# Loading order, weight layout and block schedule at the start of a fused attention and mixture-of-experts kernel

## The chip, the cores and the metric

The kernel runs on one core of a Trainium2 chip. The metric is device time in microseconds (us) of one execution, lower is better. The engines are TensorE (PE, matrix products; "PEld" in the profile is its loading of weights), VectorE (DVE), ScalarE (ACT), GpSimd (POOL) and SyncE (SP, which here only issues DMAs); ACT and POOL issue DMAs too. On each engine instructions run in program order.

## The reference

Three steps: a linear attention with a decaying state, a first feed-forward step with `h - tanh(h)`, and a second one with eight experts. Cut to what matters:

```python
# attention: batch 4, heads 8, sequence 768, head dimension 48
f = 1.0 / (1.0 + np.exp(-f_logit))
for t in range(S):
    state = f[:, :, t, :, None] * state + np.einsum('bhd,bhde->bhde', k[:, :, t], v[:, :, t])
    y[:, :, t] = np.einsum('bhd,bhde->bhe', q[:, :, t], state)
# first feed-forward step: x is 3072 x 384, w_in 384 x 2048, w_out 2048 x 384
h = x @ w_in
g = h - np.tanh(h)
x = g @ w_out
# second step: the tokens with x @ w_skip > 0 go to the best of 8 experts
# (w1 384 x 1024, w2 1024 x 384 each) and add gate_w * (relu(x @ w1[e]) @ w2[e])
```

The weights `w_in` and `w_out` arrive as 64-bit floats, seen by the kernel as pairs of 32-bit words.

## The kernel before

**Attention** goes through 24 units u; a unit is 128 tokens of one batch, u = 4 · chunk + batch, all 8 heads. For a unit SP loads `f`, `k`, `q`, `v` (L262, L275). ACT and DVE make the logarithm of the decay (exp L279, min L282, ln L286); PE sums it along the tokens (`pl`, L387); ACT takes two exponentials of that (`kp` L396, `en` L400), by which DVE scales k and q (L403, L406); PE turns both (`pk`, `pq`, L416) and ACT copies them out (`kT`, `qT`, L423). Then PE makes the scores (`ps`, L437) and adds the state's part (`py`, L446), DVE masks the scores (`A`, L460), and PE multiplies them with v ("values", L472) and makes the state's update (`pu`, L479), which DVE adds to the state S (L512). The last row of `en` goes by a DMA on ACT (L409, put_dec) to a table `dec` in DRAM; for each pair of units two DMAs (L517, on ACT) bring two rows of it back, laid out by partition, as `dd`, with which POOL decays S (L522) and DVE checks the range (`okd`, L527). `dec` is preset with ones: POOL fills `one` (L726), and SP writes it (L727), inside the first function of the program. Two units make a block of 256 tokens (`xf`), which ACT and DVE split into two parts (`xT`, L533, L537).

**First feed-forward step.** 12 blocks; the inner dimension of 2048 is 16 f-blocks of 128. For a block and an f-block: gemm1, called G (`ph`, L596, 9 matmuls), tanh (L603, ACT), the difference, called bend (L608, DVE), its split (`gs`, L613 on ACT, L619 on POOL), gemm2, called H (`po`, L636, 6 matmuls). Blocks 0, 1 and 2 run interleaved from the f-block NJOIN on; before that block 0 runs alone up to NJOIN, then 1, then 2. H of blocks 1 and 2 sums in the PSUM banks of `py` and `ps`, and waits for values 7.

**Weights.** `w_in` and `w_out` come in four quarters each (`stgw`, `stgu`, L193, two buffers in turn: w0, u0, w1, u1, ...). A quarter is decoded in four chunks of 128x768 each: |u| on ACT (L168), four steps on DVE (L170, L172, L174, L178), the high part on ACT (L339), the low part on DVE (`wlo`, `ulo`, L343). A G of f-block f needs the low part of `w_in`'s chunk f // 2. A quarter of `w_in` goes to partitions 0 to 47 and 64 to 111 (48 each) and 48 to 63 and 112 to 127 (16 each), by the order in which the heads lie in `xT`.

**What sets the order.** All instructions ahead of the last two blocks are written as steps, `step(key, due time, engine, cost, function, what it stands behind, ..., moved)`, and a planner (`in_order`, L47 to L103) emits, each time, the step that can begin first by these costs, by due time where several can. A step takes and gives PSUM buffers; each pool has two (`pa`, `yp`, `po`, `ph`). Constants: units below FIRST are prepared one by one; NJOIN, see above; CHUNK0 and CHUNK are the due times of decoding; LDAFTER is the unit behind whose q the weights may be asked for; units below ALONE take `pl` from pool `ph` and `pk`, `pq` from `po`, all others take them from `pa`, which also holds `ps` and `pu`:

```python
pl_in, pk_in = ("ph", "po") if u < ALONE else ("pa", "pa")
```

Of the kernel before, what the change touches and what calls it, by code (L numbers as in the profile page):

```python
# [92 lines left out]
def decay_attention_moe_kernel(  # L93
# [14 lines left out]
    nc = tc.nc  # L108
    P = 128
# [4 lines left out]
    NU = NCH * B  # L114
# [12 lines left out]
    AHEAD = 2  # L127
    FIRST, NJOIN, NPAY = 8, 8, 6
    EARLIEST, LEAD = -100, 28
    LDAFTER, ALONE = 4, 6  # L130
    CHUNK0, CHUNK = -75, 4
    LAG = 2
# [50 lines left out]
    def fetch(pool, name, shape, pieces, dst, eng):  # L183

        n = pieces[0][3]
        if n == 2 or dst is None:
            t = pool.tile(shape + [2], I32, tag="stg", name=f"stg{name}")
        if n == 2:
            to = t.rearrange("p a w c -> p a (w c)")
        else:  # L190
            to = t = t.bitcast(F32)[..., 0] if dst is None else dst
        for rows, a, src, _ in pieces:
            eng.dma_start(to[rows, a], src)  # L193
        return t
# [101 lines left out]

    def load_win(j):
        w = DFF // NWL
        src, m = words(w_in)
        cs = slice(j * w * m, (j + 1) * w * m)  # L300
        rows = src[:, cs].rearrange("(h r) c -> h r c", r=D)
        pieces = []
        for jj, (h0, h2, h3) in enumerate(((0, 5, 7), (4, 1, 3))):
            o = 64 * jj
            pieces.append((slice(o, o + D), slice(0, 2), rows[h0 : h0 + 3 : 2].rearrange("h r c -> r h c"), m))
            pieces.append((slice(o, o + D), slice(2, 3), rows[h2 : h2 + 1].rearrange("h r c -> r h c"), m))
            pieces.append((slice(o + D, o + 64), slice(0, 3), rows[h3].rearrange("(i r) c -> r i c", r=16), m))
        stage["w", j] = fetch(spool, f"w{j}", [P, KT, w], pieces, None, nc.sync)

    def load_wout(j):  # L310
        n = NF // NWL
        src, m = words(w_out)
        stage["u", j] = fetch(
            spool, f"u{j}", [P, n, DM],
            [(slice(0, P), slice(0, n), src[j * n * P : (j + 1) * n * P].rearrange("(f p) d -> p f d", p=P), m)],
            None, nc.sync,
        )
# [45 lines left out]
    def attend(u):  # L363
# [9 lines left out]
        def at(pos):  # L373
            return (NF * blk - LEAD if u > FIRST - 1 else EARLIEST + 12 * blk) + 6 * half + pos
# [174 lines left out]
        step(("mq", u), at(1), "DVE", 0.56, mq, ("en", u), ("q", u), ("tq", u - 2))  # L549
        step(("put_dec", u), at(1), "ACT" if u < FIRST else "SP", 0.6, put_dec, ("en", u), moved=0.1)  # L550
        step(("tk", u), at(1), "PE", 0.44, turn4("k", kp4), ("mk", u), ("init", 0), take=((pk_in, f"k{u}"),), lag=0.25)
# [163 lines left out]
    def initial():  # L715
# [10 lines left out]
        nc.gpsimd.memset(one, 1.0)  # L726
        nc.sync.dma_start(dec, one[:NU].rearrange("u p a -> u (p a)"))  # L727

# [169 lines left out]

    step(("init", 0), -400, "POOL", 3.0, initial, moved=0.1)
    step(("const", 0), 0, "POOL", 3.0, constants, ("init", 0), moved=1.0)  # L900
    step(("turn", 0), -1000, "PE", 0.4, lambda: turned.append(turn_gate()), ("const", 0), ("scores", 2), take=(("pa", "gate"),), lag=0.25)
    step(("rows", 0), -1000, "ACT", 0.5, copy_gate, ("turn", 0), give=(("pa", "gate"),))
# [8 lines left out]
    for n, (a, j) in enumerate(chunks):  # L911
        at = CHUNK0 + CHUNK * n
        if n % 2 == 0:
            step(
                ("ld", n), at - 20, "SP", 2.7 if a == "w" else 0.45, (lambda a=a, j=j: (load_win if a == "w" else load_wout)(j // 2)),
                ("stt2", n - 3), ("q", LDAFTER), moved=9.2 if a == "w" else 4.5,
            )
# [498 lines left out]
```

## Time and profile before

| | us |
|---|---|
| median of 3 runs | 752.26 (752.19 to 753.14) |
| profiled execution | 752.0 |
| its span, first to last instruction | 750.1 |
| TensorE busy in the span | 694.7 (93%) |
| VectorE busy in the span | 498.1 (66%) |

The page gives the busy time of each engine. The table of waits says for which engine or DMA an engine stood still, the timelines list single instructions with the idle time before them in brackets and what ended it, the table of stretches gives each engine's busy time between two points of the span, and the DMA view gives what the transfers of a stretch moved. "PEclk" is the clock that TensorE was granted, as a share of full speed.

### The profile page before, as it was taken

The numbers are of one execution on the slowest core, as the hardware profiler recorded it, in microseconds if no ns is written. First come the engines' busy times: TensorE is split into PE (matmuls) and PEld (weight loads), VectorE is DVE, ScalarE is ACT, GpSimd is POOL, SyncE is SP. The second block draws the span as 40 slices with busy tenths as digits, with TensorE's granted clock in tenths as the row PEclk, the third lists the DMA queues.
The fourth block names the chain that finished last, engine by engine and source line by source line (L and its number), as shares of the span: only waits on it lengthen the run. The fifth ranks groups of instructions, "written<-read, shape, count | busy, mean of one in ns | idle before, by whom it ended". The sixth has DMA issues, their size and how long they took to land. (4 is left out here: it accounts for less than half of the span.)

```text
span 750.1 us, 16375 instructions
## 1 busy us (share of the span) xinstructions
PE 694.7 (93%) x6128; PEld 655.0 (87%) x6128; DVE 498.1 (66%) x1388; ACT 366.1 (49%) x864; POOL 284.5 (38%) x317
## 2 busy tenths in 40 slices
PE   3857989999999999989999999999989989999993
PEld 2646888899998999989899999999989779999993
DVE  2448989842887947688989594955665655555530
ACT  2656575544656445554444644444333525555530
POOL 2113234443333434344343443434444214444451
PEclk9987999999999999999999999999999999999998
DMA  7978975352432223202233112005000667666500
GB/s 141 168 161 154 204 162 93 98 183 82 102 69 54 60 44 74 50 17 54 54 82 63 45 35 43 28 7 197 11 32 18 229 210 217 224 213 206 169 18 21
DMA packets 150575, 76.78 MB, mean 102 GB/s; under 512 B 116360, under 2 KB 145689, under 8 KB 150358
## 3 DMA queue, kind: packets, MB, share of 16 engines
q1 hardware_dynamic: 143318, 70.37, 37.1%
q0 software_dynamic: 2944, 5.05, 2.0%
q10 hardware_dynamic: 4224, 0.22, 0.5%
q8 instruction: 50, 0.82, 0.5%
q14 instruction: 39, 0.32, 0.1%
HBM read 61.61 MB, written 15.87 MB: 103 GB/s over the span
## 5 line engine op out<-in xcount | busy, mean ns | idle before, releaser
L619 POOL TENSOR_TENSOR gs<-th,gs 128x256 fp32r<-128x256 f32 x190 | 168.4, 889 | 240.5 <-ACT gs L613 228.2
L636 PE MATMUL po<-uhi,gs 128*128 128x384 f32 x768 | 231.0, 344 | 2.8 <-POOL gs L619 2.1
L596 PE MATMUL ph<-xT,whi 128*128 128x256 f32 x1152 | 222.4, 289 | 4.5 <-DVE th L608 4.0
L596 PEld LDWEIGHTS ph<-xT,whi 128*128 128x128 f32 x1152 | 185.8, 191 | 11.1 <-DVE th L608 7.3
L596 PE MATMUL ph<-xT,wlo 128*128 128x256 f32 x576 | 164.0, 285 | 1.7 <-DVE wlo L343 1.7
L636 PEld LDWEIGHTS po<-uhi,gs 128*128 128x128 f32 x768 | 142.7, 190 | 7.0 <-POOL gs L619 4.4
L209 DVE CUSTOM_DVE_ANT_0 scr<-pay,wb 128x384 f32<-128x384 f32 x198 | 134.2, 678 | 5.5 <-ACT pay L644 1.7
L608 DVE TENSOR_TENSOR th<-ph,th 128x256 f32<-128x256 f32 x192 | 80.1, 419 | 85.8 <-ACT th L603 84.0
L636 PE MATMUL po<-ulo,gs 128*128 128x384 f32 x384 | 130.2, 339 | 1.6 <-DVE ulo L343 1.6
L603 ACT ACTIVATE th<-ph 128x256 f32<-128x256 f32 x192 | 73.0, 381 | 118.0 <-PE ph L596 83.3
L613 ACT ACTIVATE gs<-th 128x256 fp32r<-128x256 f32 x192 | 79.6, 416 | 90.4 <-DVE th L608 85.4
L596 PEld LDWEIGHTS ph<-xT,wlo 128*128 128x128 f32 x576 | 110.8, 192 | 2.1 <-DVE wlo L343 2.1
L636 PEld LDWEIGHTS po<-ulo,gs 128*128 128x128 f32 x384 | 73.5, 191 | 2.4 <-DVE ulo L343 2.4
L1079 PE MATMUL eh<-xt,w 128*128 128x256 f32 x504 | 69.6, 283 | 0.0
L1103 PE MATMUL eo<-w,h 128*128 128x384 f32 x336 | 69.0, 342 | 0.0
L1079 PEld LDWEIGHTS eh<-xt,w 128*128 128x128 f32 x504 | 67.1, 188 | 0.4
L1103 PEld LDWEIGHTS eo<-w,h 128*128 128x128 f32 x336 | 56.3, 188 | 0.0
L1088 DVE SCALAR_TENSOR_TENSOR h<-eh,h 128x256 fp32r<-128x256 f32 x56 | 23.7, 423 | 45.1 <-ACT h L1087 45.0
L677 POOL DMA_INDIRECT xs<-pay,di x24 | 25.9, 1080 | 69.8 <-DVE sm L221 23.7
L1087 ACT ACTIVATE h<-eh 128x256 fp32r<-128x256 f32 x56 | 21.6, 386 | 61.9 <-PE eh L1079 61.8
L291 POOL TENSOR_TENSOR w<-r,w 128x768 fp32r<-128x768 f32 x24 | 43.7, 1846 | 9.1 <-ACT w L290 9.0
L437 PE MATMUL ps<-qT,kT 48*64 48x128 f32 x768 | 38.6, 288 | 7.5 <-ACT qT L423 3.9
(167 smaller groups left out, 895.4 us busy)
## 6 DMA issues: line engine op xcount, KB each, us to landing
r<-in_moe_w_dram SPq DMA_DIRECT2D x56, 384.0 KB
stgu<-in_moe_w_out_dram SPq DMA_DIRECT2D x4, 1536.0 KB
f<-in_f_logit_dram SPq DMA_DIRECT2D x24, 192.0 KB
out_dram<-pay SPq DMA_DIRECT2D x24, 192.0 KB
k<-in_k_dram SPq DMA_DIRECT2D x22, 192.0 KB
q<-in_q_dram SPq DMA_DIRECT2D x22, 192.0 KB
v<-in_v_dram SPq DMA_DIRECT2D x22, 192.0 KB
xs<-zrow SPq DMA_DIRECT2D x2, 1544.0 KB
```

The source lines that it names most:

```text
L209: nc.vector.tensor_tensor_reduce(out=scr, in0=x, in1=wb[:, n], scale=1.0, scalar=0.0, op0=ALU.mult, op1=ALU.add, accum_out=lg[:, n : n + 1])
L291: eng.tensor_tensor(lo, raw, hi.bitcast(F32), ALU.subtract)
L437: nc.tensor.matmul(ps[j][64 * a : 64 * a + 64, p * P : (p + 1) * P], lhsT=kT[r, p, 64 * a : 64 * a + 64], rhs=qT[r, p], start=True, stop=True,
L596: nc.tensor.matmul(ph, lhsT=w[:, i, fs], rhs=x[:, i, a], start=(n == 0), stop=(n == 3 * KT - 1))
L603: nc.scalar.activation(th, ph, AF.Tanh)
L608: nc.vector.tensor_tensor(th, ph, th, ALU.subtract)
L613: nc.scalar.activation(t[:, 0], th, AF.Copy)
L619: eng.tensor_tensor(t[:, 1], th, t[:, 0].bitcast(F32), ALU.subtract)
L636: nc.tensor.matmul(po[blk, s], lhsT=t[:, a, ss], rhs=w[:, f], start=(f == 0 and n == 0), stop=(f == NF - 1 and n == 2))
L677: nc.gpsimd.indirect_dma_start(xs[:, :], bass.IndirectOffsetOnAxis(ap=di[:, :], axis=0), pt[:, :], None, bounds_check=E * NT - 1, oob_is_e ...
L1079: nc.tensor.matmul(ph, lhsT=a1[:, w, i, f * P : (f + 1) * P], rhs=xt[:, i, a], start=(n == 0), stop=(n == 3 * KT - 1))
L1103: nc.tensor.matmul(eo[e, s], lhsT=h[:, a, ss], rhs=a2[:, w, f], start=(f == 0 and n == 0), stop=(f == NF2 - 1 and n == 2))
```

## The change

- The write that presets `dec` becomes a step of its own on SP, with due time -109; put_dec of each unit, and a later step (turn), now stand behind it.
- NJOIN 8 to 4, LDAFTER 4 to 3, ALONE 6 to 4, CHUNK0 -75 to -60.
- Quarter j of `w_in` was its columns 512 j to 512 j + 511. Now it is four blocks of 128 columns, at 512 w + 128 j for w = 0 to 3; rows of `w_out` likewise. The f-blocks that follow are another order of the same inner dimension. A quarter of `w_in` takes 12 DMAs with pieces of 1 KB, where it took 6 with pieces of 4 KB; the load of `w_out`'s quarter keeps its one DMA with pieces of 3 KB.
- The planner's cost of a load of `w_in` goes from 2.7 to 5.4, its transfer from 9.2 to 5.5.

PE's program has 4643 rows of instructions before and after, the same work in another order. Line numbers of the changed kernel are higher by 4, and by 8 or 9 further down.

```diff
@@ -125,10 +125,10 @@
 
 
     AHEAD = 2
-    FIRST, NJOIN, NPAY = 8, 8, 6
+    FIRST, NJOIN, NPAY = 8, 4, 6
     EARLIEST, LEAD = -100, 28
-    LDAFTER, ALONE = 4, 6
-    CHUNK0, CHUNK = -75, 4
+    LDAFTER, ALONE = 3, 4
+    CHUNK0, CHUNK = -60, 4
     LAG = 2
 
     cpool = ctx.enter_context(tc.tile_pool(name="cpool", bufs=1, side="left"))
@@ -190,7 +190,11 @@
         else:
             to = t = t.bitcast(F32)[..., 0] if dst is None else dst
         for rows, a, src, _ in pieces:
-            eng.dma_start(to[rows, a], src)
+            if len(src.shape) == 3:
+                eng.dma_start(to[rows, a], src)
+            else:
+                for i in range(src.shape[1]):
+                    eng.dma_start(to[rows, a.start + i].rearrange("p (w c) -> p w c", w=src.shape[2]), src[:, i])
         return t
 
     def load(pool, name, shape, pieces, dst):
@@ -295,16 +299,16 @@
     stage = {}
 
     def load_win(j):
+
         w = DFF // NWL
         src, m = words(w_in)
-        cs = slice(j * w * m, (j + 1) * w * m)
-        rows = src[:, cs].rearrange("(h r) c -> h r c", r=D)
+        rows = src.rearrange("(h r) (w n c) -> n h r w c", r=D, w=NWL, n=NWL)[j]
         pieces = []
         for jj, (h0, h2, h3) in enumerate(((0, 5, 7), (4, 1, 3))):
             o = 64 * jj
-            pieces.append((slice(o, o + D), slice(0, 2), rows[h0 : h0 + 3 : 2].rearrange("h r c -> r h c"), m))
-            pieces.append((slice(o, o + D), slice(2, 3), rows[h2 : h2 + 1].rearrange("h r c -> r h c"), m))
-            pieces.append((slice(o + D, o + 64), slice(0, 3), rows[h3].rearrange("(i r) c -> r i c", r=16), m))
+            pieces.append((slice(o, o + D), slice(0, 2), rows[h0 : h0 + 3 : 2].rearrange("h r w c -> r h w c"), m))
+            pieces.append((slice(o, o + D), slice(2, 3), rows[h2 : h2 + 1].rearrange("h r w c -> r h w c"), m))
+            pieces.append((slice(o + D, o + 64), slice(0, 3), rows[h3].rearrange("(i r) w c -> r i w c", r=16), m))
         stage["w", j] = fetch(spool, f"w{j}", [P, KT, w], pieces, None, nc.sync)
 
     def load_wout(j):
@@ -312,7 +316,7 @@
         src, m = words(w_out)
         stage["u", j] = fetch(
             spool, f"u{j}", [P, n, DM],
-            [(slice(0, P), slice(0, n), src[j * n * P : (j + 1) * n * P].rearrange("(f p) d -> p f d", p=P), m)],
+            [(slice(0, P), slice(0, n), src.rearrange("(w n p) d -> n p w d", n=NWL, p=P)[j], m)],
             None, nc.sync,
         )
 
@@ -547,7 +551,7 @@
         step(("en", u), at(0.5), "ACT", 0.49, en, ("ek", u), ("put_dec", u - 2), ("mq", u - 2), give=((pl_in, f"l{u}"),))
         step(("mk", u), at(1), "DVE", 0.56, mk, ("ek", u), ("k", u))
         step(("mq", u), at(1), "DVE", 0.56, mq, ("en", u), ("q", u), ("tq", u - 2))
-        step(("put_dec", u), at(1), "ACT" if u < FIRST else "SP", 0.6, put_dec, ("en", u), moved=0.1)
+        step(("put_dec", u), at(1), "ACT" if u < FIRST else "SP", 0.6, put_dec, ("en", u), ("preset", 0), moved=0.1)
         step(("tk", u), at(1), "PE", 0.44, turn4("k", kp4), ("mk", u), ("init", 0), take=((pk_in, f"k{u}"),), lag=0.25)
         step(("ck", u), at(1), "ACT", 0.59, copy4("k"), ("tk", u), ("scores", u - 2), give=((pk_in, f"k{u}"),))
         step(("tq", u), at(1.5), "PE", 0.44, turn4("q", qp4), ("mq", u), ("tk", u), take=((pk_in, f"q{u}"),), lag=0.25)
@@ -724,7 +728,11 @@
         nc.gpsimd.memset(okd, 1.0)
         one = apool.tile([P, NP, P], F32, tag="A", name="one", bufs=3)
         nc.gpsimd.memset(one, 1.0)
-        nc.sync.dma_start(dec, one[:NU].rearrange("u p a -> u (p a)"))
+
+        def preset():
+            nc.sync.dma_start(dec, one[:NU].rearrange("u p a -> u (p a)"))
+
+        turned.append(preset)
 
     def constants():
         make_upper_triangular(nc, tri_s, 1.0, diag=False)
@@ -897,8 +905,9 @@
     chunks = [(a, j + i) for j in range(0, NWC, 2) for a in "wu" for i in range(2)]
 
     step(("init", 0), -400, "POOL", 3.0, initial, moved=0.1)
+    step(("preset", 0), -109, "SP", 0.5, lambda: turned.pop()(), ("init", 0), moved=0.1)
     step(("const", 0), 0, "POOL", 3.0, constants, ("init", 0), moved=1.0)
-    step(("turn", 0), -1000, "PE", 0.4, lambda: turned.append(turn_gate()), ("const", 0), ("scores", 2), take=(("pa", "gate"),), lag=0.25)
+    step(("turn", 0), -1000, "PE", 0.4, lambda: turned.append(turn_gate()), ("const", 0), ("scores", 2), ("preset", 0), take=(("pa", "gate"),), lag=0.25)
     step(("rows", 0), -1000, "ACT", 0.5, copy_gate, ("turn", 0), give=(("pa", "gate"),))
     step(("put", 0), 0, "SP", 0.5, put_gate, ("rows", 0), moved=0.1)
 
@@ -912,8 +921,8 @@
         at = CHUNK0 + CHUNK * n
         if n % 2 == 0:
             step(
-                ("ld", n), at - 20, "SP", 2.7 if a == "w" else 0.45, (lambda a=a, j=j: (load_win if a == "w" else load_wout)(j // 2)),
-                ("stt2", n - 3), ("q", LDAFTER), moved=9.2 if a == "w" else 4.5,
+                ("ld", n), at - 20, "SP", 5.4 if a == "w" else 0.45, (lambda a=a, j=j: (load_win if a == "w" else load_wout)(j // 2)),
+                ("stt2", n - 3), ("q", LDAFTER), moved=5.5 if a == "w" else 4.5,
             )
         more = pieces(unpack(a, j))
         step(("abs", n), at, "ACT", 0.9, more, ("ld", n - n % 2), ("lo", n - 2))
```

On SP, the start of the program before (`early` are the k, q, v of units 2 and 3, and the digits behind f, k, q, v the unit):

```order
L727 DMA dec_64<-one_133 24x512
L262 DMA f0_136<-in_f_logit_dram 128x8x48
L275 DMA k0_138<-in_k_dram 128x8x48
L275 DMA q0_140<-in_q_dram 128x8x48
L262 DMA f1_142<-in_f_logit_dram 128x8x48
```

and now, where the preset stands (the queue starts with `f0` and goes on as before up to here):

```order
L279 DMA early_79<-in_q_dram 128x8x48
L279 DMA v1_153<-in_v_dram 128x8x48
L266 DMA f3_155<-in_f_logit_dram 128x8x48
L746 DMA wg_74<-in_moe2_w_gate_dram 128x3x8
L747 DMA wg_74<-in_moe2_w_skip_dram 128x3x1
L733 DMA dec_64<-one_133 24x512
L279 DMA early_79<-in_k_dram 128x8x48
```

The preset of `dec` moved from the head of the queue to behind the gate's weights `wg`. On ACT, unit 0's `en` and what followed before:

```order
L396 ACTIVATE kp0_110<-pl0_178 128x8x48
L400 ACTIVATE en0_183<-pl0_178 128x384
L409 DMA dec_64<-en0_183 8x1x48
L279 ACTIVATE f1_142<-f1_142 128x384
L423 ACTIVATE kT0_203<-pk0_188 112x512
L423 ACTIVATE qT0_206<-pq0_196 112x512
L286 ACTIVATE f1_142<-f1_142 128x384
```

and now, the rows around the same put_dec (`dec_64<-en0`):

```order
L502 ACTIVATE early_79<-py0_0_210 112x2x128
L427 ACTIVATE kT1_289<-pk1_271 112x512
L427 ACTIVATE qT1_291<-pq1_281 112x512
L283 ACTIVATE f3_155<-f3_155 128x384
L413 DMA dec_64<-en0_183 8x1x48
L413 DMA dec_64<-en1_264 8x1x48
L290 ACTIVATE f3_155<-f3_155 128x384
L521 DMA dd1_360<-dec_64 112x4x1 x2
```

Unit 0's put_dec moved from right behind `en0` to behind `kT1`, `qT1` and exp of unit 3, with unit 1's right behind it.

On SP, around quarter 0 of `w_in` (`stgw0`), before:

```order
L275 DMA v4_288<-in_v_dram 128x8x48
L262 DMA f6_295<-in_f_logit_dram 128x8x48
L275 DMA v5_375<-in_v_dram 128x8x48
L262 DMA f7_386<-in_f_logit_dram 128x8x48
L193 DMA stgw0_426<-in_moe_w_in_dram 48x2x1024
L193 DMA stgw0_426<-in_moe_w_in_dram 48x1024
L193 DMA stgw0_426<-in_moe_w_in_dram 16x3x1024
```

and now, from the second half of the quarter's 12 DMAs (the first half, the same again, stands right behind v4):

```order
L197 DMA stgw0_347<-in_moe_w_in_dram 48x4x256 x3
L197 DMA stgw0_347<-in_moe_w_in_dram 16x4x256 x3
L266 DMA f6_381<-in_f_logit_dram 128x8x48
L279 DMA v5_385<-in_v_dram 128x8x48
L266 DMA f7_393<-in_f_logit_dram 128x8x48
L194 DMA stgu0_403<-in_moe_w_out_dram 128x4x768
```

The quarter moved ahead of f6, v5 and f7, in 12 DMAs.

On DVE, from unit 3's two masks (`A3_0`, `A3_1`) to the first step of decoding (`dcw0`), before:

```order
L460 TENSOR_TENSOR A3_0_530<-ps3_0_493,tri_67 128x512
L460 TENSOR_TENSOR A3_1_536<-ps3_1_494,tri_67 128x512
L403 TENSOR_TENSOR kp0_110<-k4_193,kp0_110 128x8x48
L406 TENSOR_TENSOR qp0_112<-q4_201,en4_538 128x8x48
L282 TENSOR_SCALAR f7_386<-f7_386 128x384
L512 TENSOR_TENSOR S3_109<-pu3_549,S3_109 112x4x48
L403 TENSOR_TENSOR kp1_111<-k5_270,kp1_111 128x8x48
L406 TENSOR_TENSOR qp1_113<-q5_278,en5_625 128x8x48
L460 TENSOR_TENSOR A4_0_638<-ps4_0_597,tri_67 128x512
L460 TENSOR_TENSOR A4_1_649<-ps4_1_598,tri_67 128x512
L537 TENSOR_TENSOR xT1_670<-xf2_487,xT1_670 128x3x256
L170 TENSOR_SCALAR dcw0_672<-dcw0_672 128x768
```

and now:

```order
L464 TENSOR_TENSOR A3_0_548<-ps3_0_510,tri_67 128x512
L464 TENSOR_TENSOR A3_1_552<-ps3_1_511,tri_67 128x512
L170 TENSOR_SCALAR dcw0_546<-dcw0_546 128x768
L286 TENSOR_SCALAR f6_381<-f6_381 128x384
L172 TENSOR_SCALAR dcw0_546<-dcw0_546 128x768
L174 SCALAR_TENSOR_TENSOR dcw0_546<-stgw0_347,dcw0_546 128x768
L516 TENSOR_TENSOR S3_109<-pu3_569,S3_109 112x4x48
L178 SCALAR_TENSOR_TENSOR dcw0_546<-stgw0_347,dcw0_546 128x768
L286 TENSOR_SCALAR f7_393<-f7_393 128x384
L170 TENSOR_SCALAR dcw1_550<-dcw1_550 128x768
```

Decoding starts right behind the second mask of unit 3, ahead of unit 4's and unit 5's work on k and q that stood there.

## Rows read from the trace of the kernel before

**Rows 1.** The page: busy us, share of the span, instructions of each engine.

```profile
PE 694.7 (93%) x6128; PEld 655.0 (87%) x6128; DVE 498.1 (66%) x1388; ACT 366.1 (49%) x864; POOL 284.5 (38%) x317
```

**Rows 2.** Stretches: length; busy us (count) of PE, PEld, DVE, ACT, POOL; clock; DMA.

```profile
0.00:160.00 160.00, 127.08 (x1229) 110.78 (x1230) 114.66 (x185) 90.03 (x191) 48.77 (x76) 0.95 0.71 142
160.00:740.00 580.00, 567.64 (x4901) 544.18 (x4900) 383.40 (x1203) 276.04 (x673) 234.75 (x241) 0.99 0.32 93
```

**Rows 3.** SP's waits, 0 to 33 us: total, times, longest.

```profile
SPq L727 <- POOL tri_s masks.py:65: 3.9, 1, 3.9
...
SPq L262 <- DMA dd<-dec: 1.9, 1, 1.9
```

**Rows 4.** SP's timeline: start, duration, line, DMA, [idle before <- releaser].

```profile
4.49 0.41 SPq L727 DMA_DIRECT2D dec<-one  x1
...
4.96 0.54 SPq L262 DMA_DIRECT2D f<-in_f_logit_dram  x1
...
26.92 0.66 SPq L275 DMA_DIRECT2D v<-in_v_dram  x1
...
33.28 9.31 SPq L193 DMA_DIRECT2D stgw<-in_moe_w_in_dram  x6
```

**Rows 5.** ACT's timeline: the first of unit 3's two dd loads.

```profile
33.43 0.32 ACTq L517 DMA_DIRECT2D dd<-dec  x1
```

**Rows 6.** DVE's timeline: dd3's check, mask 3, the first decode chunk.

```profile
41.27 0.17 DVE L527 SCALAR_TENSOR_TENSOR okd<-dd,okd 112x8 f32<-112x8 f32 x1 [4.88 <-DMA dd<-dec]
...
41.65 1.28 DVE L460 TENSOR_TENSOR A<-ps,tri 128x512 f32<-128x512 f32 x2
...
54.13 0.55 DVE L170 TENSOR_SCALAR dcw<-dcw 128x768 f32<-128x768 f32 x1
...
54.71 0.56 DVE L172 TENSOR_SCALAR dcw<-dcw 128x768 int32<-128x768 int32 x1
...
55.31 0.96 DVE L174 SCALAR_TENSOR_TENSOR dcw<-stgw,dcw 128x768 int32<-128x768 int32 x1
...
56.30 0.96 DVE L178 SCALAR_TENSOR_TENSOR dcw<-stgw,dcw 128x768 int32<-128x768 int32 x1
...
58.70 0.94 DVE L343 TENSOR_TENSOR wlo<-dcw,whi 128x768 fp32r<-128x768 f32 x1
```

**Rows 7.** Stretches: mask 3 to decode, to mask 7, to the last decode step.

```profile
42.93:54.13 11.20, 9.91 (x131) 8.27 (x130) 4.85 (x11) 6.47 (x15) 1.96 (x4) 0.82 0.71 183
54.13:88.34 34.21, 26.42 (x299) 22.73 (x298) 31.88 (x49) 20.67 (x41) 8.15 (x10) 0.85 0.91 180
88.34:156.93 68.59, 63.42 (x447) 59.23 (x446) 61.94 (x95) 42.51 (x90) 29.57 (x32) 1.00 0.53 108
```

**Rows 8.** PE's timeline: first pl, values 2, 3, 5, 6, 7, G, H.

```profile
9.36 1.65 PE L387 MATMUL pl<-f,tri 128*128 128x384 f32 x2 [9.36 <-ACT f L286]
...
33.08 1.08 PE L472 MATMUL py<-A,early 128*48 128x128 f32 x15
...
42.39 2.32 PE L472 MATMUL py<-A,early 128*48 128x128 f32 x15 [4.84 <-DVE A L460]
...
64.82 1.08 PE L472 MATMUL py<-A,v 128*48 128x128 f32 x16
...
81.12 1.08 PE L472 MATMUL py<-A,v 128*48 128x128 f32 x16
...
89.30 1.08 PE L472 MATMUL py<-A,v 128*48 128x128 f32 x16
...
95.83 0.50 PE L596 MATMUL ph<-xT,whi 128*128 128x256 f32 x2 [1.50 <-DVE th L608]
...
98.08 0.34 PE L636 MATMUL po<-uhi,gs 128*128 128x384 f32 x1
```

**Rows 9.** The DMA view: a w_in quarter (37:45), then a w_out quarter (131:134.5).

```profile
DMA packets 806, 1.12 MB, mean 141 GB/s; under 512 B 533, under 2 KB 533, under 8 KB 805
...
DMA packets 443, 1.36 MB, mean 389 GB/s; under 512 B 0, under 2 KB 0, under 8 KB 443
```

## The prediction

> **What bounds the kernel now.** I read the busy shares first: TensorE (PE) is busy 93% of the span, VectorE, the next, 66% [rows 1]. By stage, PE has work for 127.1 of the first 160 us, and for 567.6 of the 580 us behind them [rows 2]. So nearly all that a re-ordering can win lies ahead of 160 us, and behind that the end moves one for one with the point at which the PE queue becomes full. PE's 4643 rows of instructions are the same after the change; I take the stretch behind 160 us, and the tail, as they are.
>
> Then the start, in three steps. SP's longest wait is for POOL's preset memset, 3.9 us, and the first load goes out at 4.96, behind the preset [rows 3, 4]. Unit 3 is the next knot: its two `dd` loads go out on ACT's queue from 33.43 [rows 5], just behind the six loads of w_in's quarter 0 that SP begins at 33.28 [rows 4], and VectorE waits 4.88 us for one of them; its mask 3 ends only at 42.93 (41.65 + 1.28) [rows 6], and PE stands 4.84 us for it [rows 8]. From there VectorE is the engine to watch: from mask 3's end to the first decode step at 54.13 it is busy 4.85 of 11.2 us, and from there to mask 7's end 31.88 of 34.21 [rows 7]. Mask 7 releases values 7 on PE at 89.30 [rows 8], the last point at which attention holds PE back; behind it PE (63.42) and VectorE (61.94) are both nearly full for 68.59 us, until decoding ends [rows 7].
>
> **The change part by part.** Units are numbered by their order; "values u" are the L472 matmuls of unit u.
>
> *1. Preset behind the first loads.* `f0` is now SP's first instruction and can go out when SP is ready, at 4.49 − 3.90 = 0.6 us, where it went out at 4.96: units 0 and 1 start 4.4 us earlier, pl at about 5.0 where it was 9.36 [rows 3, 4, 8]. The preset now stands behind `wg`, and both decay rows (put_dec 0 and 1) stand behind ACT's exp of unit 3, as the order shows; the dd loads of unit 1 stand behind these, and pl 2 and pl 3 go behind values 1 on PE. Followed through the new order with the durations of rows, values 2 comes at about 32.9, before 33.08 [rows 8]. So I cost this part at 0: the head start is spent ahead of values 2. Bounds: if none is spent, −4.4; if the later put_dec makes one more queue wait for a `dd` to land as SP does once, 1.9 us [rows 3], +2.
>
> *2. Unit 3's dd loads.* Quarter 0 of w_in is now asked for right behind v4; f6, v5 and f7, which stood ahead of it on SP, stand behind it. Before, its bytes were on the move when dd was asked for: 141 GB/s from 37 to 45 [rows 9], 1.57 MB in some 11 us. After, it can begin behind v4, at some 27 us (26.92 + 0.66 [rows 4], with nothing gained from part 1); only its last three small pieces wait for a put_dec at 33 to 34. So dd finds the queue nearly empty and lands at 36.5 to 38 instead of 41.27. Then not dd but en of unit 4 comes last for scores 3 (below, ALONE), at 37.8, and mask 3 ends at 39.2: **−3.8**, and values 3 comes at 38.6 instead of 42.39. Bounds: 0 (dd waits for the quarter as before), −4.9 (the whole wait).
>
> *3. Decoding fills VectorE's hole.* The quarter is there at 36 to 39, so the first decode step stands right behind mask 3, where before 11.2 us lay between [rows 7]. I counted VectorE's work between mask 3 and mask 7 in the new order with rows' durations (a decode chunk is 0.55 + 0.56 + 0.96 + 0.96 and 0.94 for `wlo`, 3.97 us [rows 6]): 35.4 us, where it was 36.7 (4.85 + 31.88). Fewer decode steps stand there (20, not 23), more bends (7, not 4). Before, the 45.4 us were 81% filled, the decode part of them 93% [rows 7]. I take 89%, since decoding is now there throughout but pa's turns (below) will leave holes: 35.4/0.89 = 39.8, less 45.4: **−5.6**. Bounds: 81% gives −1.7, 93% −7.3. Mask 7 then ends at 39.2 + 39.8 = 79.0, and values 7 comes at 79.9 instead of 89.30.
>
> *4. Three blocks on each chunk.* With blocks 1 and 2 joining at the fifth step, a decoded chunk feeds three blocks. In the new PE order nine gemm1 groups stand ahead of values 7, where six stood. One is 1.12 us (two from 95.83 to 98.08 [rows 8]), so PE has 3 × 1.12 = **−3.3** less to do behind it; before, PE stood idle there. gemm2's groups ahead of it are four in both.
>
> *5. Behind values 7.* The same sum for VectorE gives 57.7 us of work up to the last decode step (58.2 before, for which the row has 61.94), so 61.4. PE's work is 63.42 − 3.3 = 60.1. Before, PE was the longer of the two; now VectorE is, and a stretch of 68.59 − 3.3 = 65.3 would need it 94% busy, where it was 90%, and 93% at most in any row here [rows 7]. At 91.5% it takes 67.1: **+2** (bounds 0 and +3). Quarter 2 of w_in lands at 95 to 98 and is wanted at 98 to 99.5: 0, at worst +2. For waits of order that I do not see, **+1.5**.
>
> [...]
>
> *7. w_in by 128-column blocks.* Twelve loads with pieces of 1 KB, not six with 4 KB: 24 more SP issues over the kernel, on an engine whose queue waits anyway; 0. The time of a quarter is unknown. Its rows' shape, 48 and 16 partitions, is as before, and it moved at 141 GB/s; w_out's, over 128 partitions in pieces of 3 KB, moved at 389 [rows 9]. At 389 a quarter would take 4.0 us, at 141 11. I take 11, the row of its own shape. Quarter 0 has the time for it (27 to 39), the others are asked for up to 15 us ahead.
>
> [...]
>
> Sum: 0 − 3.8 − 5.6 − 3.3 + 2 + 1.5 + 1.5 = **−7.7**, with the numbered parts in order. The profiled execution took 752.0 (span 750.1 and 1.9 around it), 0.26 below the median 752.26, so 744.3 + 0.26, about **744.5**.
>
> **The rivals.** *(a) The late quarters come late.* If a quarter of twelve small loads takes 13 us instead of 11 (each load waits for a shared completion lane, and W0's stand in a row with dd and put_dec), quarters 2 and 3 miss their places by 2 us together and dd waits for half of quarter 0: 744.5 + 2 ≈ 746.5. For it: the 141 GB/s is far below what the chip moved elsewhere [rows 9]. Against: SP asks earlier.
>
> *(b) The early gain is eaten.* ACT's queue now holds put_dec 0 and 1 and the dd loads in one row ahead of unit 2's copies, and v5 and f7 stand behind quarter 0 on SP. If mask 3 ends at 42.9 as before, part 2 is gone: 752.3 − 3.9 ≈ 748.4.
>
> *(c) Slower: two banks for four units.* Units 4 and 5 took pl, pk and pq from the banks of `ph` and `po`; now, with ALONE at 4, they queue with scores in the two banks of `pa`, each freed by an ACT or VectorE operation that stands among decode steps. Unit 6, which ran so already, took 16.3 us from values 5 (64.82) to values 6 (81.12), unit 7 8.2 [rows 8]. My sum has 41.3 us for four units, 10.3 each. The gain is gone when values 7 comes at 87.6 (the +1.7 of parts 4 to 6 then eats the rest), that is at 12.3 each. With two units at 16.3 and two at 10.3 it comes at 91.8: 752.3 + 2.5 + 1.7 ≈ 756.5; with all four at 16.3, 768. Against: unit 6's 16.3 had four gemm1 and several gemm2 groups and pieces of a half clock in it, which fill PE.
>
> *(d) It does what it says and no more:* parts 2 and 3 at their lower bounds, 0 and −1.7, with part 4, and costs as summed: 752.3 − 1.7 − 3.3 + 5 = 752.3, no change.
>
> **How the numbers follow.** Forecast 0.60 (its own range 738.5 to 748), (a) 0.14, (b) 0.11, (d) 0.06, (c) 0.09. What a measurement of this kernel can tell from no change is about 0.2%, 1.5 us. Forecast, (a) and (b) are faster: 0.85, of which I take 0.03 for their upper edges; (d) and that edge give same 0.07; (c) and a share of (d), 0.11. The low end, 738.5, has parts 2 and 3 at their best with a third of the costs of parts 5 and 6: 752.3 − 4.9 − 7.3 − 3.3 + 1.7. The high end, 750.5, is (b) with (a)'s 2 us on top; (c), (d) and little more are left out.
>
> **What would show it.** In the changed profile: the first pl near 5 us; SP without the 3.9 us wait; `dd` of unit 3 released by 38 and mask 3 ending near 39; VectorE's first decode step within 2 us of it; values 7 near 80; nine gemm1 groups ahead of it; PE's idle time ahead of 160 us down from 32.9 (160 − 127.1) to about 25; quarter loads near 11 us. Wrong if PE's waits name `pl`, `pk` or `pq` of units 4 to 7 (c), or if waits for `wlo` and `ulo` behind 90 exceed 5 us (a).

## The result, and the profile after

The changed kernel took 741.72 us (median of 4 runs, 739.64 to 742.59) where the kernel before took 752.23 beside it: a ratio of 0.9862, 95% interval 0.9829 to 0.9896, or 10.5 us gained. The profiled execution took 741.21, its span is 739.0 (before: 752.0 and 750.1). A repeat (e11, below) gave 740.76 and a ratio of 0.9852.

First the stretches of [rows 2], now of the changed kernel (length; busy us and count of PE, PEld, DVE, ACT, POOL; clock; DMA share; GB/s):

```profile
0.00:160.00 160.00, 135.94 (x1294) 118.55 (x1295) 115.74 (x184) 92.38 (x197) 55.42 (x81) 0.97 0.69 146
160.00:740.00 580.00, 556.31 (x4836) 533.86 (x4834) 383.45 (x1204) 273.16 (x668) 231.09 (x236) 0.99 0.32 92
```

PE has 8.9 us more work behind it at 160 us (135.94, not 127.08), and correspondingly less to do behind that. The gain lies in the early part, as forecast. How it got there differs from the forecast. SP's timeline, where [rows 4] stood:

```profile
0.74 0.44 SPq L266 DMA_DIRECT2D f<-in_f_logit_dram  x1
...
12.46 0.44 SPq L733 DMA_DIRECT2D dec<-one  x1
...
23.57 15.08 SPq L197 DMA_DIRECT2D stgw<-in_moe_w_in_dram  x12
```

The first load goes out at 0.74 and the preset is the fifteenth load of the queue, where SP does not wait for POOL (before: 3.9 us [rows 3]); quarter 0 of `w_in` goes out at 23.57, 9.7 us earlier than before and 3.4 earlier than I had it. The rows of ACT (unit 3's `dd` loads, then the first step of decoding) and of VectorE (`okd`, mask 3, the first decode step), which answer to [rows 5, 6]:

```profile
36.60 0.85 ACTq L521 DMA_DIRECT2D dd<-dec  x2
...
41.03 1.72 ACT L168 ACTIVATE dcw<-stgw 128x768 f32<-128x768 f32 x2
```

```profile
40.26 0.15 DVE L531 SCALAR_TENSOR_TENSOR okd<-dd,okd 112x8 f32<-112x8 f32 x1
...
41.25 1.29 DVE L464 TENSOR_TENSOR A<-ps,tri 128x512 f32<-128x512 f32 x2 [0.83 <-PE ps L441]
...
42.45 0.55 DVE L170 TENSOR_SCALAR dcw<-dcw 128x768 f32<-128x768 f32 x1
```

The `dd` loads are issued at 36.60, 3.2 us later than before, and VectorE does not wait for them here; but mask 3 ends at 42.54 (41.25 + 1.29), where it ended at 42.93. What is new stands behind it: the first decode step at 42.45, before 54.13. PE's first `pl` and values 2 to 7, for [rows 8]:

```profile
6.69 1.65 PE L391 MATMUL pl<-f,tri 128*128 128x384 f32 x2 [6.69 <-ACT f L290]
...
35.30 0.42 PE L476 MATMUL py<-A,early 128*48 128x128 f32 x2
...
42.57 1.09 PE L476 MATMUL py<-A,early 128*48 128x128 f32 x16
...
52.15 1.95 PE L476 MATMUL py<-A,v 128*48 128x128 f32 x16
...
64.46 1.08 PE L476 MATMUL py<-A,v 128*48 128x128 f32 x16
...
73.90 1.08 PE L476 MATMUL py<-A,v 128*48 128x128 f32 x16
...
84.39 1.08 PE L476 MATMUL py<-A,v 128*48 128x128 f32 x16
```

Values 2 is 2.2 us later than before, values 3 0.2 later, values 7 4.9 earlier (84.39, before 89.30). How far this goes for one profile only is seen from the repeat e11, the same program:

```profile
33.13 0.42 PE L476 MATMUL py<-A,early 128*48 128x128 f32 x2
...
39.98 0.17 DVE L531 SCALAR_TENSOR_TENSOR okd<-dd,okd 112x8 f32<-112x8 f32 x1 [1.85 <-DMA dd<-dec]
```

There values 2 is at 33.13, as before, VectorE waits 1.85 us for `dd`, mask 3 ends at 41.34, and values 3 and 7 come at 41.38 and 82.46. So single points of the start move by 1 to 2 us between executions of the same program.

The first `pl` is 2.7 us earlier, though `f0` goes out 4.2 us earlier. Ahead of unit 0's min on VectorE stands an instruction that waits for POOL:

```profile
5.42 0.17 DVE L744 CAST iota<-io 128x8 f32<-128x8 int32 x1 [2.77 <-POOL io L743]
```

It starts at 5.42 in both kernels. Unit 0's exp was done after that before (at 8.35), and is done ahead of it now (at 4.12), so the min waits.

Last the stretches from mask 3's end to mask 7's end and on to the last decode step, for [rows 7]:

```profile
42.54:84.28 41.74, 36.60 (x460) 31.61 (x459) 35.30 (x59) 28.15 (x62) 14.25 (x17) 0.92 0.87 193
84.28:153.78 69.50, 65.55 (x456) 60.77 (x455) 62.86 (x89) 41.25 (x86) 29.98 (x33) 1.00 0.50 96
```

VectorE has 35.30 us of work in the first one (before 36.73 in 45.41 us) and PE 36.60 (36.32 before). In the second PE is busy 65.55 of 69.50, idle for 3.95; before it was idle for 5.17 of 68.59.

### The profile page after: what moved, and what is told of

It reads as the page before. It is cut to its first block, busy times and chain, and to the rows that moved or that the text cites. A ratio compares the mean times of both kernels' runs of the same rounds, so it can differ in the third digit from the quotient of the medians.

```text
span 739.0 us, 16409 instructions
## 1 busy us (share of the span) xinstructions
PE 692.2 (94%) x6128; PEld 652.4 (88%) x6128; DVE 499.2 (68%) x1388; ACT 365.5 (49%) x864; POOL 286.5 (39%) x317
## 5 line engine op out<-in xcount | busy, mean ns | idle before, releaser
L213 DVE CUSTOM_DVE_ANT_0 scr<-pay,wb 128x384 f32<-128x384 f32 x198 | 131.1, 662 | 5.6 <-ACT pay L648 1.7
L1097 DVE SCALAR_TENSOR_TENSOR h<-eh,h 128x256 fp32r<-128x256 f32 x56 | 23.6, 421 | 44.6 <-ACT h L1096 44.4
L838 POOL DMA_INDIRECT out_dram<-yo,xa x16 | 15.7, 983 | 72.5 <-DVE yo L846 37.3
```

The costliest lines, as they stand in the source:

```text
L213: nc.vector.tensor_tensor_reduce(out=scr, in0=x, in1=wb[:, n], scale=1.0, scalar=0.0, op0=ALU.mult, op1=ALU.add, accum_out=lg[:, n : n + 1])
L1097: nc.vector.scalar_tensor_tensor(out=h[:, 1], in0=ph, scalar=0.0, in1=h[:, 0].bitcast(F32), op0=ALU.max, op1=ALU.subtract)
```

## The experiments

Every time below is a median. Since the kernel before itself came out at 751.4 to 752.6, I compare by the ratio to it on the same chip; the last column is that ratio in us of 752. The changed kernel stands at 0.9862, or -10.4, and 0.9852.

| run | edit | us | ratio (95%) | by the ratio |
|---|---|---|---|---|
| e1 | changed, quarters contiguous | 744.90 | 0.9888 (0.9853 to 0.9924) | -8.4 |
| e2 | changed, NJOIN 8 | 750.27 | 0.9970 (0.9945 to 0.9996) | -2.3 |
| e3 | changed, preset first | 748.75 | 0.9950 (0.9931 to 0.9970) | -3.8 |
| e4 | before, NJOIN 4 | 747.64 | 0.9948 (0.9926 to 0.9969) | -3.9 |
| e5 | changed, SP starts late | 748.59 | 0.9941 (0.9915 to 0.9967) | -4.4 |
| e6 | changed, less decoding | 739.35 | 0.9829 (0.9791 to 0.9867) | -12.9 |
| e7 | changed, preset tenth, not fifteenth | 748.13 | 0.9939 (0.9916 to 0.9961) | -4.6 |
| e8 | before, preset moved | 748.75 | 0.9965 (0.9935 to 0.9995) | -2.6 |
| e9 | changed, quarter 0 late | 744.24 | 0.9894 (0.9854 to 0.9934) | -8.0 |
| e10 | before, less decoding | 747.36 | 0.9925 (0.9895 to 0.9955) | -5.6 |
| e11 | changed again | 740.76 | 0.9852 (0.9821 to 0.9882) | -11.1 |
| e12 | changed, LDAFTER 1 | 747.66 | 0.9949 (0.9928 to 0.9970) | -3.8 |

My theory at the start was that order makes the gain: decoding fills VectorE's hole behind mask 3, and three blocks on each chunk give 3.3 us more. The rivals were the quarter's smaller pieces, the head start itself, and three blocks as the main cause.

### e2 and e4: three blocks on each chunk

```diff
-    FIRST, NJOIN, NPAY = 8, 4, 6
+    FIRST, NJOIN, NPAY = 8, 8, 6
```

and in e4 the opposite edit on the kernel before.

> The changed kernel with blocks 1 and 2 joining at the ninth step again. If my sum is right, three blocks on a chunk are worth the three gemm1 groups alone, 3.3 us: 745 us. If feeding three blocks is the main cause (PE then has six groups for each chunk pair and does not wait for decoding), 6 to 8 us are lost: 748 to 750, and PE's waits for wlo, ulo and bend ahead of 105 us come back, 5 us or more.

> The kernel before with nothing changed but that blocks 1 and 2 join at the fifth step. My sum: 3.3 us gained, 749 us. If feeding three blocks is the main cause: 6 to 8 us gained, 744 to 746 us.

Undoing it costs 8 to 9 us of 10.4 to 11.1; doing it alone gains 3.9 by the ratio and 5.0 by the medians. Together with the rest it is worth more than twice my 3.3. PE's timeline of e2 shows how (values 7, then the first gemm1 group that waits):

```profile
84.35 2.33 PE L476 MATMUL py<-A,v 128*48 128x128 f32 x15 [1.99 <-DVE A L464]
...
92.67 0.50 PE L600 MATMUL ph<-xT,whi 128*128 128x256 f32 x2 [2.74 <-ACT whi L343]
```

Values 7 comes at 84.35, at the same time as in the changed kernel (84.39), with attention and decoding moved up just as well. But four gemm1 groups stand ahead of it where the changed kernel has nine, and behind it PE waits 2.74 us for `whi` of the next chunk. The two spans differ by 8.2 us (747.2 and 739.0). Five groups at 1.12 are 5.6 of it. For the rest, the stretches from values 7 to 160 us of e2 and of the changed kernel:

```profile
84.35:160.00 75.65, 69.62 (x480) 66.65 (x481) 63.54 (x94) 44.24 (x93) 34.50 (x36) 0.96 0.59 131
```

```profile
84.39:160.00 75.61, 71.66 (x499) 66.99 (x499) 63.95 (x91) 43.65 (x92) 33.04 (x37) 1.00 0.52 112
```

PE stands idle 2.1 us longer (6.03 and 3.95), and its clock is 0.96 in the mean, not 1.00; values 7 itself takes 2.33 us and not 1.08. Together this is more than the remaining 2.6 us, and the two were not taken apart. In e4 eleven groups stand ahead of values 7 instead of six, 5.6 us, and values 7 itself is 1.8 later. Both edits let the planner plan anew. The fourteen profiles of this document agree with them: from values 7 to the end of the span it is 652.5 to 656.4 us in the nine that join at the fifth step and decode all, and 659.1 to 662.9 in before, e8 and e2, which join at the ninth; with less decoding it is 653.3 in e6 (fifth) and 653.9 in e10 (ninth).

### e3, e8 and e5: the preset and the head start

e3 puts the preset back to the head of SP's queue, by which the planner also moves other steps; e8 moves it alone, in the kernel before. e5 keeps the changed kernel's order on every engine and only starts SP later:

```diff
+        if u == 0:
+            nc.gpsimd.memset(fx[u][:, :1], 0.0)
         nc.sync.dma_start(
             fx[u].rearrange("t (h d) -> t h d", h=H), ...
```

> The changed kernel with the preset of the decay rows first on SP's queue again. If the head start is spent ahead of values 2, as I forecast: within 1.5 us of the changed kernel, 740.2 to 743.2, values 3 no later than now. If the head start counts: the 2.7 us by which the first pl moved are lost, 744.4.

> The kernel before with the preset as a step of its own at its new due time, nothing else changed. If the head start is spent at once: 751 to 753.5. If it is worth its 2.7 to 4.4 us: 748 to 749.6.

> The changed kernel, every instruction in the same order, but the first load's target gets one narrow POOL memset behind the preset's, so that SP starts some 4 us later, as in the kernel before. If the head start is spent ahead of values 2 (my part 1): within 1.5 us of the changed kernel, 741 to 743, values 3 within 1 us of 42.6. If the head start itself is worth something: 2.7 us (the first pl's shift) to 4 us lost, 744.4 to 745.7; then the 7 us that the preset's undoing cost in e3 are 3 to 4 of order.

I expected e3 and e5 to lose nothing; against the changed kernel they lose 6 to 8 us, more than either of the cases written down for them, and e8 gains 2.6 (interval 0.4 to 4.9). Yet the attention does not show it: in e5 values 3 comes at 43.08, 0.5 us behind the changed kernel. The loss comes afterwards. SP's timeline of e5 (quarter 0), ACT's (first step of decoding) and PE's (values 3, `pq` of unit 4, values 4):

```profile
31.13 11.59 SPq L197 DMA_DIRECT2D stgw<-in_moe_w_in_dram  x12
```

```profile
47.25 1.68 ACT L168 ACTIVATE dcw<-stgw 128x768 f32<-128x768 f32 x2 [5.87 <-DMA stgw<-in_moe_w_in_dram]
```

```profile
43.08 1.09 PE L478 MATMUL py<-A,early 128*48 128x128 f32 x16
...
50.13 1.10 PE L422 MATMUL pq<-ident,qp 128*112 128x128 f32 x4 [5.51 <-ACT kT L429]
...
60.15 1.95 PE L478 MATMUL py<-A,v 128*48 128x128 f32 x16
```

Quarter 0 goes out at 31.13 instead of 23.57: besides its later start, SP stands 3.2 us ahead of it for a `dd` to land, which it does not do in the changed kernel ahead of the quarter. ACT then stands 5.87 us for the quarter at its first |u|. Its next instructions in program order are copies that the attention needs, `kT` of unit 4 among them, so PE stands 5.51 us, and values 4 comes at 60.15, where the changed kernel has it at 52.15. So in e5 the head start is lost through the weights' arrival, and an in-order engine hands the wait on.

In e8, where the quarter keeps its pieces of 4 KB, the head start is spent in another place. Quarter 0 goes out at 27.45, 5.8 us earlier than before, and ACT's copy behind the `dd` loads waits for unit 3's put_dec, which went out at 30.08:

```profile
39.62 0.28 ACT L494 ACTIVATE tm<-py 112x128 f32<-112x128 f32 x1 [5.33 <-DMA dec<-en]
```

Values 3 of e8 comes at 44.82, 2.4 us later than before.

### e9: the quarter, and what stands behind it on SP, comes late

```diff
     def load_win(j):
+        if j == 0:
+            for i in range(8):
+                nc.sync.dma_start(spare[:, i], f_logit[0, i, :P, :8])
```

> The changed kernel with eight loads of 4 KB each (read by nobody) on SP right ahead of w_in's quarter 0: every other engine's program is the same, the attention starts as early as in the changed kernel, and only the quarter and SP's queue behind it go out some 4 us later. If the head start is worth its 7 us through the quarter's arrival (ACT's first decode step stands ahead of unit 5's kT): 4 us or more lost, 745.5 or above, the first |u| later than 45, values 3 unchanged near 42. If the attention's own earlier start is the gain: the same as the changed kernel, 741 to 743.

The attention starts as early as in the changed kernel. SP's timeline (the eight loads that nobody reads, then the quarter) and ACT's first |u|:

```profile
23.85 5.42 SPq L305 DMA_DIRECT2D spare<-in_f_logit_dram  x8
...
29.31 11.36 SPq L197 DMA_DIRECT2D stgw<-in_moe_w_in_dram  x12
```

```profile
44.46 1.69 ACT L168 ACTIVATE dcw<-stgw 128x768 f32<-128x768 f32 x2 [3.78 <-DMA stgw<-in_moe_w_in_dram]
```

3.5 us are lost against the repeat e11 beside it by the medians (744.24 and 740.76), 3.2 by the ratios: a little under the 4 that I asked for, with the first |u| at 44.46 where I asked for 45, and the two intervals overlap (0.9854 to 0.9934, 0.9821 to 0.9882). Values 3 is at 42.38 and PE stands 3.17 us for ACT's `kT` (of unit 4; the text above calls it unit 5). Four of the runs that have the same order on PE, VectorE, ACT and POOL line up by the start of the first |u| in their profiles: 40.29 (e11, 740.8), 41.03 (the changed kernel, 741.7), 44.46 (e9, 744.2), 47.25 (e5, 748.6). About one us is lost for each us that it is late. Two more runs have this order and are left out: e6, which has less work (40.53, 739.4), and e1 (42.92, 744.9), 1 to 2 us above that line; it loses time in another place (next section). So the rival that the attention's own earlier start makes the gain falls, as far as four runs of e9 and one profile can tell.

### e1: the quarters contiguous, same order

```diff
-        rows = src.rearrange("(h r) (w n c) -> n h r w c", r=D, w=NWL, n=NWL)[j]
+        cs = slice(j * w * m, (j + 1) * w * m)
+        rows = src[:, cs].rearrange("(h r) c -> h r c", r=D)
```

with `w_out` and the loads likewise as before.

> The changed kernel with w_in's and w_out's quarters contiguous again (6 loads with pieces of 4 KB for a quarter of w_in), every instruction else in the same order. First theory (the gain comes from order: decoding behind mask 3 and three blocks on each chunk): the same as the changed kernel, 740.5 to 743 us. Second theory (smaller pieces bring the quarter sooner): 3 us or more is lost, 745 or above, and quarters show over 11 us against under 9.

The time lies 2 to 4 us above the changed kernel, between what the two theories asked for, but single runs go from 742.3 to 748.8 and the intervals overlap, so the size is open; the profiled run is the slowest. Smaller pieces do not bring a quarter sooner. From 92 to 100 us, inside a quarter, and from 130 to 134, inside one of `w_out`, the changed kernel's DMA view has

```profile
DMA packets 1193, 1.11 MB, mean 138 GB/s; under 512 B 114, under 2 KB 1193, under 8 KB 1193
...
DMA packets 475, 1.45 MB, mean 362 GB/s; under 512 B 4, under 2 KB 4, under 8 KB 475
```

so 138 GB/s with pieces of 1 KB, about the 141 with 4 KB [rows 9], and 362 over 128 partitions: here the pieces do not set the rate. What differs is a small transfer that runs beside them. ACT's timeline of e1, put_dec of unit 3, the `dd` loads and the copy behind them:

```profile
32.16 0.65 ACTq L409 DMA_DIRECT2D dec<-en  x1
...
34.96 5.22 ACTq L517 DMA_DIRECT2D dd<-dec  x2
...
40.22 0.28 ACT L494 ACTIVATE tm<-py 112x128 f32<-112x128 f32 x1 [4.75 <-DMA dec<-en]
```

The second `dd` load cannot be issued before unit 3's put_dec has landed, and ACT stands 4.75 us for that with 4 KB pieces of the quarter on the move; 1.5 KB issued at 32.16 arrive past 39. In the changed kernel put_dec goes out at 32.52 and both `dd` loads by 37.45, and ACT does not wait for it. It does not land at once there either; SP's waits from 23.6 to 39:

```profile
SPq L197 <- DMA dec<-en: 3.6, 1, 3.6
SPq L197 <- DMA dd<-dec: 3.2, 2, 2.3
```

SP, which sends quarter 0, stands 3.6 us for that put_dec and sends the quarter's next load at 36.80. So unit 3's put_dec took 4.3 us in the changed kernel (32.52 to 36.8), and in all profiles with pieces of 1 KB the second `dd` load goes out at most 5.7 us behind it (e9: 30.85 and 36.54). With pieces of 4 KB beside it, it took 7.6 in e1 (32.16 to 39.8) and 9.2 in e8 (30.08 to 39.25). Values 3 of e1 comes at 46.46. The two profiles with 4 KB pieces on the move thus lose about 5 us on ACT in this place; that the pieces are the cause, and nothing else in the order of the bytes, was not shown.

### e6 and e10: VectorE's load behind values 7

```diff
+        if short:
+            c, ci, v = c[:, :1, :8], ci[:, :1, :8], v[:, :1, :8]
         nc.vector.scalar_tensor_tensor(
             out=ci, in0=v, scalar=29, in1=ci, op0=ALU.logical_shift_right, op1=ALU.bitwise_or
```

with `short` for chunks 4 to 7 of both weights; their lowest bits stay zero.

> The changed kernel with the fourth VectorE step of decoding cut to 8 columns in chunks 4 to 7 of w_in and of w_out (the lowest bits of those weights stay zero): 7.7 us less VectorE work behind values 7, same order. If VectorE bounds that stretch (my part 5: 2 us lost there): 2 us or more faster than the changed kernel, 739.7 or below. If PE has enough other work there, so that decoding ends early for nothing: the same, 741 to 743.

> The kernel before with the same cut as e6 (7.7 us less VectorE work in chunks 4 to 7). If VectorE's load behind values 7 cost the kernel before as much as it costs the changed one: 1.5 to 3.5 us faster than before. If three blocks on a chunk brought a new cost by VectorE (my part 5): no gain here, within 1 us of before, and the gain only in e6.

Less decoding gains 5.6 us in the kernel before (interval 3.4 to 7.9) and 1.7 in the changed one (e6 against e11), where the intervals overlap, so that a gain is not told from none; the median of 739.35 is under the 739.7 that I asked for, which stood on the first measurement, 741.72. The 5.6 us lie above the range that I had for e10. So three blocks on a chunk brought no new cost by VectorE: its load cost the kernel before no less than the changed one, and probably more. PE's waits behind values 7 (us in total, times, longest), of the kernel before, of e10 and of the changed kernel:

```profile
PE ph L596 <- DVE th L608: 2.0, 4, 1.5
PE po L636 <- POOL gs L619: 1.4, 2, 0.7
PE ph L596 <- DVE wlo L343: 0.7, 1, 0.7
PE po L636 <- DVE ulo L343: 0.6, 1, 0.6
```

```profile
PE ph L598 <- DVE th L610: 1.5, 1, 1.5
PE ph L598 <- DVE wlo L345: 0.7, 1, 0.7
PE po L638 <- DVE ulo L345: 0.6, 1, 0.6
```

```profile
PE po L640 <- POOL gs L623: 1.9, 4, 0.8
PE ph L600 <- DVE th L612: 1.1, 4, 0.4
PE po L640 <- ACT gs L617: 1.0, 1, 1.0
```

Before, PE waits 4.7 us here, 1.3 of them for `wlo` and `ulo`; the changed kernel has none of these, and 4.0 in all. Part 5 had the sign of the change wrong: the waits for decoding did not grow, they went. Where e10 gains is shown in part: 1.9 us of waits are gone in its profile, and a clock stretch (next section); the waits for `wlo` and `ulo` stayed.

### e7 and e12: two tries to go further

e7 tells the planner that filling `one` needs no transfer; e12 lets the weights go behind q of unit 1.

```diff
-    step(("init", 0), -400, "POOL", 3.0, initial, moved=0.1)
+    step(("init", 0), -400, "POOL", 3.0, initial)
```

```diff
-    LDAFTER, ALONE = 3, 4
+    LDAFTER, ALONE = 1, 4
```

> The changed kernel with the planner told that the preset's fill needs no transfer time, which puts the preset eighth on SP behind v0 and the gate's weights, put_dec 0 and 1 in their old places on ACT and pl 2 earlier. If the late values 2 (35.3 where I forecast 32.9) came from put_dec and pl 2 standing late: values 2 near 31, values 3 near 40, 739 us. If the order elsewhere decides: anything from 738 to 746, values 3 not earlier than 42.

> The changed kernel with the first quarter allowed behind q of unit 1 (LDAFTER 1): quarter 0 then stands behind q4 on SP, ahead of f5, and the first chunk's decoding stands ahead of mask 3. If the quarter's arrival is what counts and VectorE has room ahead of mask 3: |u| of chunk 0 by 37, values 7 earlier by 2 to 4 us, 738 to 740. If f5 and v4 behind twelve loads, or decoding ahead of mask 3, hold the attention back: 743 to 748.

Both lose 6 to 7 us. In e7 the preset is the tenth load (the text above has it eighth). Values 2 and 3 come at 33.29 and 41.42, earlier than in the changed kernel's first profile, but no earlier than in its repeat (33.13 and 41.38), so that nothing shows put_dec and `pl` 2 to have made them late. The order behind them is another one, values 4 comes at 53.79 and values 7 at 90.60, and the time lies above all that I had for it; which of its many moves costs that was not taken apart. In e12 the quarter goes out at 18.38 and the first |u| starts at 38.35, but now twelve loads and the `dd` loads of unit 1 meet. ACT's copy of unit 1 (behind the `dd` issues) and PE's values 2:

```profile
26.91 0.28 ACT L498 ACTIVATE early<-py 112x128 f32<-112x128 f32 x1 [4.06 <-DMA dd<-dec]
```

```profile
37.39 0.42 PE L476 MATMUL py<-A,early 128*48 128x128 f32 x2
```

ACT stands 4.06 us for `dd`, values 2 comes at 37.39 and the head start is gone. In this plan, then, an earlier quarter is no gain: it meets the round trips of `dec`. Neither kernel beats the changed one.

## Why the prediction came out right, and where its steps did not

The time lies in the range, and two of the mechanisms that carried it were in the prediction: decoding in VectorE's hole, and three blocks on each chunk. That the number came out so near is luck, since two misses offset each other. Values 7 came at 84.39 where I had 79.9, 4.5 us too late; and behind values 7 the kernel gained 6.2 us where I had a loss of 1.7. Point by point:

- **Part 1 (preset, 0): wrong.** I followed the head start through the attention alone, where it is indeed spent: values 2 comes at 35.30 and, in the repeat, 33.13 (before 33.08; I had 32.9). The first `pl` came at 6.69, not 5.0. I missed that SP's queue carries the head start on to quarter 0, which I let go out at 27 "with nothing gained from part 1"; it went out at 23.57. e5 loses 6 to 8 us by a late start alone.
- **Part 2 (dd, -3.8): wrong.** The 4.88 us wait for `dd` is gone, as forecast, but `dd` is issued later, values 2 is late, and mask 3 ends 0.4 us earlier, not 3.7 (in the repeat 1.85 us of the wait are left, and mask 3 ends 1.6 earlier). Here rival (b) is what happened. Its price of 3.9 is most of the 4.5 us by which values 7 was late; the gain behind values 7 hid it. I also had only the quarter's last three loads wait for a put_dec; SP stood 3.6 us for that, 3.2 for `dd` loads, and its twelve loads took 15.08 us.
- **Part 3 (VectorE's hole, -5.6): right in size,** with 35.30 us of work (I had 35.4), filled to 85% (89). From values 3 to values 7 it is 41.8 us (41.1 in the repeat) where I had 41.3 and before had 46.9. The quarter that I had at 36 to 39 is decoded from 41.03 on; this cost nothing because mask 3 was late as well. And it hangs on part 1: with the quarter late (e5) it takes 49.6 (92.64 - 43.08).
- **Part 4 (three blocks, -3.3): right in its count, too small as a cause.** Nine groups stand ahead of values 7. Against what the same early part would do without them (e2) it is five groups, 2.1 us of standing and a lower clock, 8.2 us in the spans.
- **Parts 5 and 6 (+5): wrong sign.** From values 7 to the end it took 6.2 us less (span less values 7: 654.6, before 660.8), of which 3.3 are part 4, so the rest is -2.9, where I had +5. A chunk that feeds three blocks gives PE work for longer, so that VectorE may be 90% busy (62.86 of 69.50) without PE waiting for decoding; I took a busy share for a bound. The last +1.5 of the sum, for the clock (part 6), is shown by no run: the granted clock is 1.00 from 84.28 on, as it was before from 88.34 on [rows 7]. 1.2 us less idle time is in the rows above. Some 1.7 more is a clock stretch that the profile of before has and that of after does not. The stretch 320 to 340 of before, and 310 to 330 of after, at the same place of the program:

```profile
320.00:340.00 20.00, 17.98 (x155) 17.23 (x154) 18.22 (x62) 11.30 (x26) 9.34 (x11) 0.91 0.09 31
```

```profile
310.00:330.00 20.00, 18.01 (x165) 17.20 (x164) 19.37 (x68) 12.07 (x28) 9.91 (x12) 1.00 0.09 31
```

The mean clock is 0.91 and 1.00; 0.09 of 20 us are 1.8. The profiles of e4, e8 and e10, all made from the kernel before, show 1.00 there too, so this is most likely a thing of that one run and no gain of the change.

- **Part 7 (a quarter's time unchanged): right in the rate,** 138 GB/s and 141, **not in the time of quarter 0:** from its first load to the first |u| it was 17.5 us (23.57 to 41.03), and 15.2 and 16.1 in e9 and e5, where ACT stood for it, where I had 11 to 12. So the 3.4 us that it went out earlier were spent again. What smaller pieces do for a small transfer beside them was not in my list.

The losses of e2, e3 and e1 add up to more than the whole gain, as they would if the parts need each other: blocks that join early need chunks, and chunks need the quarter. ALONE and CHUNK0 were not tried apart, nor LDAFTER at its old value.

From the start to the end: +0.2 at values 3, -5.1 to values 7, -6.2 behind: -11.1 in the spans, -10.5 in the medians, against -7.7. Of the rivals, (a) came by its mechanism at quarter 0 alone, whose loads stood in a row with `dd` and put_dec (SP waited 3.2 and 3.6 us for them); the late quarters cost nothing, there is no wait for `wlo` or `ulo` behind 90. (c) did not come: units 4 to 7 took 9.6, 12.3, 9.4 and 10.5 us, and PE's longest wait for `pk` among them is 1.49; in unit 6's 16.3 us of before the granted clock was 0.50 from 75 to 77.5.

## What to carry to other kernels

When a head start seems to be spent, follow every queue that it runs through, not only the chain of compute: here SP's queue carried it to a weight load, whose arrival an in-order engine turned into waits of the attention (in e5 ACT stood 5.87 us, and PE 5.51 behind it). A busy share near 90% need not be a bound: look who waits for the engine. Here, feeding three blocks from each decoded chunk removed the waits for decoding at the same share (61.94 of 68.59 us before, 62.86 of 69.50 now; e2 has 3.2 us of them, the changed kernel none behind values 7). And where a planner sets the order, test a cause with the order held fixed (e1, e5, e9), since an edit that lets it plan anew (e3, e7, e12, and e2, e4, e8 too) may move several us by itself. Take a second profile of the same program before reading 1 or 2 us off one.

## What I had not expected of the hardware

- 1.5 KB written by one queue beside a quarter in pieces of 4 KB took 7.6 us to land (e1) and 9.2 (e8), and ACT stood for it; beside pieces of 1 KB, at about the same rate (138 and 141 GB/s), it took 4.3 in the changed kernel, where SP stood for it, and at most 5.7 in the others.
- The same program's time spread over some 3 to 6 us: 739.2 to 743.7 for the changed kernel (e11, 6 runs), 742.3 to 748.8 for e1. It goes with the clock that the runs were granted in the mean: 0.989 and 0.988 in the two fastest of e11, 0.980 in its slowest; 0.987 at 743.4 us and 0.977 at 749.5 in e10.
